# Gated linear attention and a feed-forward layer: keys and queries transposed into scratch tiles in token pairs, growth products over alpha

## The chip, the core and the metric

The kernel runs on one core of a Trainium2 chip. The metric is device time in microseconds (us), the median of several runs. Besides, one execution was taken with the hardware profiler; all views of the profile come from that one execution.

## The reference

Attention comes first, for 4 batches, 8 heads, 768 tokens and a head size of 48, and a feed-forward layer over its 3072 tokens (width 384, hidden width 2048) follows:

```python
for t in range(S):
    state = alpha[:, :, t, :, None] * state + einsum('bhd,bhe->bhde', k[:, :, t], v[:, :, t])
    y[:, :, t] = einsum('bhd,bhde->bhe', q[:, :, t], state)
x = y.transpose(0, 2, 1, 3).reshape(B * S, H * D)
h = x @ w_in
g = h * clip(h + 3.0, 0.0, 6.0) / 6.0
out = g @ w_out
```

The inputs arrive as float64, handed over as their bits, and the chip turns the weights into fp32. alpha lies between 0.8 and 1. All products are fp32.

## The kernel before

**Chunks.** Attention is worked in 24 chunks of 128 tokens, six to a batch. Inside a chunk the recurrence becomes products: keys are multiplied by decay products R (of all alphas from a token to the chunk's end), queries by growth products P. R comes from a scan over alpha backwards (`decay`, L309), followed by a small reciprocal of its first column into a tile `ini` (L313). P comes from a forward scan over alpha that starts from `ini` (`growth`, L320). Both scans run on VectorE. Heads are held in four pairs; alpha, `ini` and P lie as four runs of W = 129 floats, the first of each run being a zero in alpha (the start of the run, which the scan resets at), and `ini` holding a value there and zeros elsewhere.

**Getting the tokens into the free dimension.** alpha, k and q must have tokens along the free dimension. The first six chunks are turned by TensorE (L282). From chunk 6 on (`FIRST`), loads put each of them into a "quad" tile in an order of tokens by which VectorE's transposes of 32 x 32 blocks do the turning (`by_blocks`, L286): four blocks v of a quad are written interleaved, token u of block v to place 4u + v, so that each write goes 16 bytes beyond the last. Then `scaled` (L332) multiplies k by R and q by P, in place, in the tiles `Ks` and `Qs`, of which there are two each, taken in turns by chunk. Keys are needed by token too: `turn_k` (L391) transposes the scaled keys in blocks back into the quad tile, and SyncE's queue writes that to DRAM (`write_k`, L396) and reads it back in another order (`read_k`, L404).

**The rest of a chunk.** Scores are TensorE products of scaled keys and queries (L346), masked by VectorE (L356); ScalarE copies the queries beside them (`place_q`, L366; it does nothing for the first half of a batch's first chunk). GpSimd (POOL) decays the state (L409) by R's first column, ScalarE places it beside the values (L419), TensorE makes the update (L430), VectorE the next state (L438, L440), TensorE the outputs (L456), and ScalarE copies them (L465) to be the feed-forward layer's input.

**Feed-forward.** Two chunks are a group, of which there are twelve. The first groups use plain products (L479, L490, L517), the gate by ScalarE (L495) and VectorE (L499). From the third group on they use products in fewer multiplications: sums of blocks by VectorE (L540, L542, L544, L650, L667), TensorE products (L603 and L706), and ScalarE copies of what is kept (L609).

**Weights.** In the first 80 us or so, the weights are converted: among the steps, ScalarE (L186), VectorE (`high_bits`, L203 to L210, whose last operation reads and writes the odd words of pairs of 32-bit words), and an add on POOL (`add_low`, L217). Loads of the first two quads of each kind are preceded by small memsets on POOL (L257).

**Order.** All the work is issued in one order, written out by hand as a list of words, each a step with its arguments. Each engine runs its instructions in that order, and waits where its data or its tile isn't ready. Words that matter here: `r.j` decay, `p.j` growth, `tk.j` and `tq.j` the transposes of keys and queries, `k.j` and `q.j` the multiplies, `kt.j`, `kw.j` and `kr.j` the way of the keys through DRAM, `st.j` the decayed state on POOL, `sm.j` next state, `sv.j` placing it, `qa.j` placing queries, `la`, `lk`, `lq` loads of alpha, k and q, `d3.i` and `d4.i` the weights' high bits and POOL add, `fr` and `fg` gate steps on ScalarE and VectorE, `xc.g`, `o.g`, `s.g`, `M.g`, `P.g` sums and products of a feed-forward group. `b` is the plain second product, `ca.j` the transpose of alpha, `n.g` a kept copy. A chunk's `tk`, `k`, `kt`, `tq` and `q` stand among the feed-forward words of earlier groups.

Of the kernel before, what the change touches and what calls it, by code (L numbers as in the profile page):

```python
# [8 lines left out]
FP = mybir.dt.float32  # L9
# [8 lines left out]
def kernel(  # L18
# [86 lines left out]
    aX, ini = [], []  # L105
    for r in range(2):
        t = consts.tile([C, NP * W + 1], FP, tag=f"ax{r}")
        nc.vector.memset(t, 0.0)
        aX.append(t)
        t = consts.tile([C, NP * W], FP, tag=f"ini{r}")  # L110
        nc.vector.memset(t, 0.0)
        ini.append(t)
# [114 lines left out]
    Ps = consts.tile([C, NP * W], FP, tag="P", name="P")  # L227
# [46 lines left out]
    def transposed(name, j, i=None):  # L274
        if j >= FIRST:
            t = (K_t if name == "k" else Q_t)[j] = (Ks if name == "k" else Qs)[j % 2]
            by_blocks(t, name, j)
            return
        t = bank("t" + name, j, i)
        src = ring[name, j % NR]  # L280
        for p in range(NP):
            nc.tensor.transpose(  # L282
                t[:, p], src[:, 2 * p : 2 * p + 2].rearrange("s h d -> s (h d)"), ident)

    def by_blocks(to, name, j):
        nc.vector.transpose(out=to.rearrange("r p (u v) -> r p v u", v=V),  # L286
                            in_=quads[name, j % NQ][:, :, :, 0:BLK])
# [16 lines left out]
    def decay(j):  # L304

        n = NP * W
        ax, ic = aX[j % 2], ini[j % 2]
# [5 lines left out]
        nc.vector.reciprocal(out=ic.rearrange("r (p w) -> r p w", w=W)[:, :, 0:1],  # L313
                             in_=R_t[j][:, :, 0:1])

    def growth(j):

        n = NP * W
        P_t[j] = Ps
        nc.vector.tensor_tensor_scan(  # L320
            out=P_t[j], data0=aX[j % 2][:, 0:n], data1=ini[j % 2], initial=0.0,
            op0=ALU.mult, op1=ALU.add)

    def scaled(name, j):

        if j < FIRST:
            src = ps_t.pop(("t" + name, j))
            t = (Ks if name == "k" else Qs)[j % 2]
        else:
            src = t = (K_t if name == "k" else Q_t)[j]  # L330
        by = R_t[j][:, :, 1:W] if name == "k" else without_first(P_t.pop(j))
        nc.vector.tensor_tensor(out=t, in0=src, in1=by, op=ALU.mult)  # L332
        (K_t if name == "k" else Q_t)[j] = t
# [423 lines left out]
    with tc.manual_schedule():  # L757
# [16 lines left out]
               f.1.7.0 r.6 f.1.3.3 d4.8 d2.4 w.10 tk.5.3 d4.9 w.11 dx.4 fr.1.7.1 sm.4.0 d3.4 w.12  # L774
               d2.10 qa.4.0 fg.1.7 fr.1.3.1 m.4 lq.5 d1.10 f.1.6.0 d3.10 d1.12 d4.4 fr.1.0.0 f.1.2.1
               p.5 fg.1.3 d2.12 k.5 fg.1.0 d3.12 d4.10 fr.1.6.1 sm.4.1 tq.5.1 sv.4.1 lk.6 w.13
# [37 lines left out]
               kw.11 M.4.11 G.3.2.1 h.4.0 tq.11 e.4.1.1 la.13 sm.10.1 tk.12 qa.12.0 sv.10.1 M.4.18.0  # L814
               P.3.4 n.4.18.12 q.11 kr.11 sv.12.0 M.4.19 G.3.1.3 o.4.6.0 n.4.11.8 M.4.12 o.4.5.0
               st.11 k.12 qa.10.1 u.11.0 lq.12 h.4.1 qa.11.1 sv.11.0 sm.11.0 tq.12 sc.11.1.2 sv.11.1
               la.14 n.4.12.14 kt.12 P.3.6 M.4.6.2 qa.11.0 o.4.3.0 G.3.3.2 M.4.13 m.11 n.4.13.14
               ca.13 kw.12 ya.11.1 yb.11 cy.11 ya.10.2 o.4.2.0 qa.18.0 o.4.2.1 e.4.2.1 o.4.3.1 yb.10
               M.4.15.1 p.12 cy.10 M.4.16 q.12 xc.5.1 M.4.14 e.4.3.0 xc.5.0 xc.5.3 o.4.4.0 lk.13
               O.3.3 xc.5.4 h.4.3 xc.5.5 kr.12 O.3.1 P.4.0.2 M.5.0.0 o.4.6.1 xc.5.6 e.4.4.0 xc.5.7  # L820
               xc.5.2 M.4.17 h.4.4 lv.13.2 h.4.2 e.4.5.0 n.5.0.14 o.4.7.0 e.4.6.1 u.12.3.0 sc.12.3.0
# [27 lines left out]
               O.5.3 M.7.2 sc.16.3.2 u.16.3.0 qa.16.1 r.17 k.17 r.18 n.7.2.11 G.6.0.0 M.7.3 kt.17  # L849
               h.6.5 M.7.4 n.7.4.15 s.6.1.9 O.4.1 P.6.3.0 tk.18 qa.16.0 s.6.2.12 xc.7.10 M.7.5 K.6.2  # L850
               kw.17 s.6.4 o.7.0.0 k.18 sm.16.0 la.19 s.6.3.8 n.7.5.9 M.7.9 e.7.0.0 kr.17 tq.17
               P.6.2 M.7.18.2 o.7.1.0 sv.16.1 p.17 s.6.5 lk.19 kt.18 O.5.1 M.7.10 sm.16.1 q.17 P.6.5
# [4 lines left out]
               n.7.13.8 o.7.2.0 M.7.16 cy.17 G.6.1.2 cy.16 xc.8.1 M.7.14 q.18 xc.8.3 lq.19 xc.8.4  # L857
               xc.8.10 o.7.6.1 o.7.2.1 e.7.6.1 xc.8.5 e.7.2.0 P.6.6 xc.8.6 G.6.3.1 o.7.4.0 xc.8.0
               xc.8.7 h.7.6 O.5.2 xc.8.8 M.8.0.3 M.7.17 M.8.7.1 O.6.1 o.7.7.1 h.7.2 sm.18.0 n.8.0.11
               n.8.7.8 M.8.1 e.7.3.1 n.8.1.12 r.19 e.7.7.0 xc.8.9 sm.18.1 P.7.0.0 k.19 la.20 K.7.0.2  # L860
               st.19 lk.20 M.8.8 la.21 tq.19 h.7.7 M.8.2 h.7.3 n.8.2.9 e.7.4.1 h.7.4 kt.19 lv.19.0
               sv.19.0 P.7.1 s.7.0.14 M.8.3 M.8.4 G.7.0.2 s.7.1.10 P.7.3.2 xc.8.2 s.7.2.13 kw.19
               n.8.4.15 o.8.0.0 M.8.9 s.7.3.14 kr.19 lk.21 p.19 ca.20 P.7.2 la.22 o.8.1.0 q.19
               e.8.0.1 M.8.10 O.6.3 sc.18.1.3 sc.19.2.0 u.19.1.3 s.7.5 qa.18.1 s.7.4 K.7.2 K.7.1
               tk.20 e.8.1.0 n.8.10.10 h.8.0 M.8.5 lq.20 sv.18.1 lq.21 M.8.11 n.8.11.14 P.7.5
               qa.19.1 M.8.12 h.8.1 sm.19.0 ca.21 n.8.12.9 m.18 n.8.5.13 P.7.4 r.20 qa.19.0 tq.20
               m.19 lv.20.1 M.8.6.3 sv.19.1 M.8.13 G.7.2.1 M.8.18.2 ya.18.2 n.8.13.15 k.20 o.8.3.0
               tk.21 sm.19.1 n.8.18.9 G.7.1.3 ya.19.1 yb.18 yb.19 O.7.2 o.8.3.1 kt.20 o.8.2.0 cy.19
               cy.18 M.8.14 e.8.3.1 o.8.2.1 xc.9.1 O.7.0 h.8.3 P.7.6 xc.9.3 xc.9.4 G.7.3.2 o.8.6.0
               xc.9.0 xc.9.5 M.8.15.3 e.8.2.1 la.23 xc.9.6 o.8.6.1 xc.9.10 st.20 e.8.6.0 o.8.7.0  # L870
               xc.9.7 M.8.16 kw.20 xc.9.8 M.9.0.0 h.8.6 P.8.0.1 kr.20 o.8.4.0 xc.9.9 n.9.0.15 p.20
               O.7.3 M.8.19 e.8.4.0 q.20 h.8.2 lk.22 M.9.1 h.8.4 o.8.5.0 M.8.17 qa.20.0 u.20.1.2
               n.9.1.9 e.8.5.0 o.8.7.1 e.8.7.1 h.8.5 sc.20.1.0 r.21 M.9.7.2 K.8.0.3 sm.20.0 M.9.2
               P.8.1 h.8.7 n.9.7.13 n.9.2.8 sm.20.1 s.8.0.10 G.8.0.1 sv.20.0 M.9.3 p.21 s.8.1.12
               M.9.8 sv.20.1 s.8.2.11 M.9.4 m.20 tk.22 n.9.4.14 k.21 P.8.3.3 o.9.0.0 kt.21 qa.20.1
               xc.9.2 e.9.0.0 s.8.4 M.9.5 st.21 h.9.0 M.9.9 s.8.3.14 o.9.1.0 K.8.2 tq.21 P.8.2 ca.22
               kw.21 lq.22 s.8.5 lv.21.0 kr.21 q.21 n.9.5.12 r.22 K.8.1 M.9.18.0 M.9.10 qa.21.0
               P.8.5 e.9.1.1 n.9.18.14 lv.23.2 sv.21.0 p.22 G.8.2.2 tq.22 ca.23 O.6.0 k.22 kt.22
               n.9.10.10 r.23 qa.21.1 P.8.4 M.9.11 u.21.3.2 sc.21.1.0 n.9.11.11 M.9.15.3 sm.21.0
               M.9.12 G.8.1.0 lk.23 ya.20.3 yb.20 m.21 sm.21.1 sv.21.1 h.9.1 tk.23 n.9.12.8 o.9.6.0  # L880
               cy.20 ya.21.1 yb.21 M.9.19 o.9.5.0 kw.22 M.9.16 M.9.13 o.9.3.0 M.9.6.0 O.8.0 o.9.4.0
               cy.21 n.9.13.8 xc.10.1 e.9.4.1 M.9.17 xc.10.3 o.9.7.0 q.22 lv.22.1 o.9.3.1 qa.22.1
               M.9.14 P.8.6 qa.22.0 st.22 kr.22 xc.10.0 u.22.1.2 O.8.1 o.9.2.0 xc.10.4 G.8.3.1
               o.9.2.1 e.9.3.0 xc.10.5 o.9.7.1 h.9.3 o.9.6.1 e.9.2.0 xc.10.10 h.9.4 M.10.0.0 O.8.2
               n.10.0.8 xc.10.6 P.9.0.1 M.10.1 e.9.7.1 K.9.0.3 xc.10.8 h.9.2 k.23 xc.10.7 e.9.6.0
               h.9.6 e.9.5.0 s.9.0.13 P.9.1 n.10.1.9 kt.23 h.9.5 h.9.7 sm.22.0 O.8.3 M.10.7.2 lq.23
               G.9.0.0 s.9.1.12 sv.22.0 M.10.2 P.9.3.3 s.9.4 s.9.2.10 n.10.2.14 xc.10.2 M.10.3 kw.23
               tq.23 sv.22.1 s.9.3.13 s.9.5 O.7.1 M.10.4 kr.23 p.23 n.10.7.11 M.10.8 P.9.2 n.10.4.15
               q.23 K.9.1 sm.22.1 o.10.0.0 K.9.2 M.10.9 u.23.3 sc.23.1.0 o.10.1.0 qa.23.0 sc.22.3.2
               m.22 M.10.10 P.9.4 st.23 sm.23.0 n.10.10.12 M.10.11 n.10.11.10 e.10.1.0 e.10.0.1  # L890
               M.10.5 h.10.0 P.9.5 qa.23.1 n.10.5.15 G.9.1.1 M.10.12 P.9.6 n.10.12.13 o.10.3.0
               M.10.13 xc.10.9 sv.23.1 G.9.3.2 G.9.2.3 m.23 M.10.15.0 M.10.6.1 n.10.13.13 M.10.18.3
               h.10.1 M.10.16 o.10.2.0 O.9.3 n.10.18.13 o.10.7.0 o.10.2.1 o.10.3.1 sv.23.0 ya.22.3
               yb.22 ya.23.2 yb.23 cy.22 cy.23 e.10.3.1 o.10.6.0 o.10.4.0 O.9.1 xc.11.1 M.10.14
               M.10.19 o.10.6.1 e.10.2.0 o.10.5.0 h.10.2 xc.11.3 M.10.17 e.10.5.0 xc.11.4 O.9.2
# [45 lines left out]
```

## Time and profile before

| | before |
|---|---|
| Median of 3 runs | 533.77 us (533.75 to 533.82) |
| Profiled execution, own time | 533.63 us |
| Its span | 531.82 us |
| TensorE matmul busy | 524.3 us (99%) |
| TensorE weight load busy | 494.0 us (93%) |
| VectorE busy | 475.6 us (89%) |
| ScalarE busy | 261.4 us (49%) |
| GpSimd (POOL) busy | 50.3 us (9%) |
| Granted TensorE clock | 1.00 throughout |

The span is from the first to the last instruction; 1.81 us of the execution's own time lie outside it. In the profile PE is TensorE's matmul, PEld its weight load, DVE VectorE, ACT ScalarE, POOL GpSimd and SP SyncE, whose queue issues the transfers; L12 is line 12 of the kernel. A group gives line, engine, operation, output and input tiles by name, shapes and count, then busy time and the mean of one in ns, then the idle time before and what ended it. A line of the timeline gives start, duration, engine, line, operation and, in brackets, the idle time before it with what ended that. Tiles are called by the names in the program: `q<-qq` is a transpose from a quad of queries, `kq<-k` the one of `turn_k`, `k<-k,R` a multiply, `t_ps` and `m_ps` are PSUM.

### The profile page before, as it was taken

The numbers are of one execution on the slowest core, as the hardware profiler recorded it, in microseconds if no ns is written. First come the engines' busy times: TensorE is split into PE (matmuls) and PEld (weight loads), VectorE is DVE, ScalarE is ACT, GpSimd is POOL, SyncE is SP. The second block draws the span as 40 slices with busy tenths as digits, with TensorE's granted clock in tenths as the row PEclk, the third lists the DMA queues.
The fourth block names the chain that finished last, engine by engine and source line by source line (L and its number), as shares of the span: only waits on it lengthen the run. The fifth ranks groups of instructions, "written<-read, shape, count | busy, mean of one in ns | idle before, by whom it ended". The sixth has DMA issues, their size and how long they took to land.

```text
span 531.8 us, 15076 instructions
## 1 busy us (share of the span) xinstructions
PE 524.3 (99%) x6290; PEld 494.0 (93%) x6290; DVE 475.6 (89%) x839; ACT 261.4 (49%) x513; POOL 50.3 (9%) x71
## 2 busy tenths in 40 slices
PE   8999999999999999999999999999999999999997
PEld 5798886789999999999999999999999999999997
DVE  7999999999999999999999999998999999486471
ACT  4888875212664453542673554544454454443330
POOL 5333353100000100000000000000000000000000
PEclk9999999999999999999999999999999999999999
DMA  9999867005363253453463553443531532010000
GB/s 177 246 241 251 247 153 177 2 2 133 74 150 84 64 118 77 115 123 89 95 156 85 120 136 91 96 107 69 145 78 20 129 98 48 1 33 7 9 17 30
DMA packets 124100, 54.40 MB, mean 102 GB/s; under 512 B 83328, under 2 KB 116864, under 8 KB 124032
## 3 DMA queue, kind: packets, MB, share of 16 engines
q1 hardware_dynamic: 124032, 53.44, 42.2%
q8 instruction: 49, 0.80, 0.7%
q14 instruction: 19, 0.16, 0.1%
HBM read 44.50 MB, written 8.91 MB: 100 GB/s over the span
## 4 chain that ended last, share of the span: by engine, by line
PE 85%; DVE 7%; ACT 4%; DMA 1%; issue 1%; SPq 1%; POOL 0%; DVEq 0%; ACTq 0%
PE m_ps L706 36%; PE m_ps L603 31%; PE m_ps L479 4%; PE m_ps L517 4%; PE t_ps L456 4%; PE t_ps L346 2%; PE t_ps L430 2%; DMA rings<-in_q_dram 1%; DVE A L356 1%; ACT A L366 1%; DVE g_sb L540 1%; ACT r L495 1%; ACT raw L186 1%; DVE g_sb L499 1%; SPq L251 1%
## 5 line engine op out<-in xcount | busy, mean ns | idle before, releaser
L706 PE MATMUL m_ps<-w,g_sb 128*128 128x192 f32 x704 | 121.7, 326 | 0.0
L609 ACT COPY g_sb<-m_ps 128x512 f32<-128x512 f32 x110 | 63.5, 584 | 104.2 <-PE m_ps L603 86.4
L706 PEld LDWEIGHTS m_ps<-w,g_sb 128*128 128x128 f32 x704 | 113.7, 190 | 0.6 <-DVE g_sb L667 0.3
L706 PE MATMUL m_ps<-rings,g_sb 128*128 128x192 f32 x528 | 91.7, 327 | 0.2 <-DVE g_sb L650 0.2
L706 PEld LDWEIGHTS m_ps<-rings,g_sb 128*128 128x128 f32 x528 | 85.3, 190 | 0.6 <-DVE g_sb L650 0.5
L603 PE MATMUL m_ps<-xc,w 128*128 128x128 f32 x640 | 83.5, 277 | 0.0
L603 PEld LDWEIGHTS m_ps<-xc,w 128*128 128x128 f32 x640 | 77.9, 192 | 1.1
L495 ACT ACTIVATE r<-g_sb,half 128x512 f32<-128x512 f32 x80 | 57.0, 722 | 29.8 <-DVE g_sb L499 11.9
L499 DVE SCALAR_TENSOR_TENSOR g_sb<-r,g_sb 128x512 f32<-128x512 f32 x80 | 53.5, 682 | 8.7 <-ACT r L495 8.4
L603 PE MATMUL m_ps<-xT,raw 128*128 128x128 f32 x400 | 52.8, 277 | 0.0
L603 PEld LDWEIGHTS m_ps<-xT,raw 128*128 128x128 f32 x400 | 48.8, 192 | 0.5 <-ACT g_sb L609 0.2
L409 POOL TENSOR_TENSOR st<-sm,R 128x192 f32<-128x192 f32 x20 | 12.6, 630 | 358.2 <-DVE sm L440 300.5
L650 DVE TENSOR_TENSOR g_sb<-g_sb 128x512 f32<-128x512 f32 (+1 forms) x55 | 42.1, 792 | 3.7 <-PE m_ps L706 3.5
L603 PE MATMUL m_ps<-xT,w 128*128 128x128 f32 x320 | 42.0, 277 | 0.0
L603 PEld LDWEIGHTS m_ps<-xT,w 128*128 128x128 f32 x320 | 39.0, 192 | 0.4
L366 ACT COPY A<-q 48x256 f32<-48x256 f32 x88 | 35.4, 403 | 7.3 <-DVE q L332 6.1
L356 DVE TENSOR_TENSOR A<-t_ps,mask 64x256 f32<-64x256 f32 x96 | 36.2, 416 | 1.2 <-PE t_ps L346 0.8
L479 PE MATMUL m_ps<-xT,w 128*128 128x256 f32 x144 | 33.3, 384 | 0.5 <-POOL w L217 0.3
L603 PE MATMUL m_ps<-xc,raw 128*128 128x128 f32 x240 | 32.1, 277 | 0.1
L479 PEld LDWEIGHTS m_ps<-xT,w 128*128 128x128 f32 x144 | 26.5, 190 | 5.3 <-POOL w L217 0.9
L540 DVE TENSOR_TENSOR g_sb<-g_sb 128x512 f32<-128x512 f32 x40 | 27.2, 682 | 4.6 <-ACT g_sb L609 4.6
L309 DVE TENSOR_TENSOR_SCAN R<-t,ones 128x516 f32<-128x516 f32 x24 | 29.6, 1233 | 1.6 <-ACT t L300 1.6
(105 smaller groups left out, 726.9 us busy)
## 6 DMA issues: line engine op xcount, KB each, us to landing
raw<-in_moe_w_out_dram SPq DMA_DIRECT2D x8, 768.0 KB, 5.5
raw<-in_moe_w_in_dram SPq DMA_DIRECT2D x6, 768.0 KB, 7.3
v<-in_v_dram SPq DMA_DIRECT2D x48, 96.0 KB, 3.1
out_dram<-oh SPq DMA_DIRECT2D x44, 96.0 KB, 1.8
far<-kq SPq DMA_DIRECT2D x64, 64.0 KB, 2.2
kb<-far SPq DMA_DIRECT2D x64, 64.0 KB, 2.0
aq<-in_alpha_dram SPq DMA_DIRECT2D x36, 96.0 KB, 2.5
kq<-in_k_dram SPq DMA_DIRECT2D x36, 96.0 KB, 2.5
```

Source lines behind the costliest of these rows:

```text
L309: nc.vector.tensor_tensor_scan(out=reverse(R, n - 1, n), data0=reverse(ax, n, n), data1=reverse(ones, n, n), initial=0.0, op0=ALU.mult, op ...
L356: nc.vector.tensor_tensor(out=to[:, a], in0=sc[a][half], in1=mask[half, half].unsqueeze(1).to_broadcast([HB, NP, HB]), op=ALU.mult)
L366: nc.scalar.copy(out=to[:, a], in_=Q_t[j][64 * a : 64 * a + D, :, half])
L456: nc.tensor.matmul(y_of(j, (i + 1) // 2, p)[:, HB * b : HB * b + HB], vb[:, p, e : e + 32], A_t[j][:, b, 2 * p + a], start=(b == 0 and i = ...
L479: nc.tensor.matmul(h[:, f], w1[:, kk, o : o + C], xT_t[g][:, kk], start=(kk == 0), stop=(kk == KT - 1))
L495: nc.scalar.activation(out=to, in_=h, func=AF.Relu, bias=half, scale=1.0 / 6.0)
L499: nc.vector.scalar_tensor_tensor(out=to, in0=r, scalar=1.0, in1=h, op0=ALU.min, op1=ALU.mult)
L540: eng.tensor_tensor(out=out, in0=in0, in1=in1, op=ALU.add if s1 > 0 else ALU.subtract)
L603: nc.tensor.matmul(acc[g][i][:, f * C : (f + 1) * C], spots[w][:, f * C : (f + 1) * C], x_of(g, x), start=(first and f == 0), stop=last, s ...
L609: nc.scalar.copy(out=slots[z], in_=acc[g][i])
L650: nc.vector.tensor_tensor(out=out, in0=in0, in1=in1, op=ALU.subtract)
L706: nc.tensor.matmul(to[g], a, rhs[:, f], start=(first and f == 0), stop=(last and f == HF - 1), skip_group_check=True)
```

## The change

1. `tk.j` and `tq.j` of chunks 6 on no longer write `Ks` and `Qs` but scratch tiles (`turns`), one for keys and one for queries. In scratch the tokens lie in two halves, w = 0 and 1, which are 1 KB apart; each half holds pairs (4u + 2w, 4u + 2w + 1), so that a transpose writes every second float, 8 bytes beyond the last.
2. The multiplies of these chunks read scratch in pairs (two floats, then two from the other half), the growth or decay products and the output `Ks` or `Qs` contiguously in the same order.
3. The growth scan of chunks 6 on writes over its input alpha; chunks before that write the queries' scratch tile, and the tile P of its own is gone. Since the scan overwrites the four zeros that start the runs of alpha, a memset of 4 columns on POOL follows each such scan (18 of them) and sets them to zero again.
4. There is one `ini` tile in place of two, and one memset less at the start. So growth j must be issued before decay j + 1, and multiply k.j before tk.(j + 1).
5. The list of words is the same up to the places of some: r.6 moves behind p.5; r.18 and k.18 move behind p.17, ahead of s.6.5; tk.22 moves behind k.21; qa.12.0 and qa.18.0, which do nothing, move too. TensorE's and ScalarE's own orders stay as they were.

```diff
-    aX, ini = [], []
+    aX = []
     for r in range(2):
         t = consts.tile([C, NP * W + 1], FP, tag=f"ax{r}")
         nc.vector.memset(t, 0.0)
         aX.append(t)
-        t = consts.tile([C, NP * W], FP, tag=f"ini{r}")
-        nc.vector.memset(t, 0.0)
-        ini.append(t)
+    ini = consts.tile([C, NP * W], FP, tag="ini")
+    nc.vector.memset(ini, 0.0)
...
-    Ps = consts.tile([C, NP * W], FP, tag="P", name="P")
+    places = {name: consts.tile([C, NP * W], FP, tag=f"{name}t", name=f"{name}t")
+              for name in "kq"}
+    turns = {name: t[:, 0 : NP * C].rearrange("r (w p n) -> r w p n", w=2, p=NP)
+             for name, t in places.items()}
...
     def transposed(name, j, i=None):
         if j >= FIRST:
-            t = (K_t if name == "k" else Q_t)[j] = (Ks if name == "k" else Qs)[j % 2]
-            by_blocks(t, name, j)
+            nc.vector.transpose(
+                out=turns[name].rearrange("r w p (u b) -> r p w b u", b=V // 2),
+                in_=quads[name, j % NQ].rearrange("r p (w b) d -> r p w b d", w=2)[..., 0:BLK])
             return
...
     def growth(j):
-        P_t[j] = Ps
-        nc.vector.tensor_tensor_scan(
-            out=P_t[j], data0=aX[j % 2][:, 0:n], data1=ini[j % 2], initial=0.0,
-            op0=ALU.mult, op1=ALU.add)
+        P_t[j] = places["q"] if j < FIRST else aX[j % 2]
+        to = P_t[j][:, 0:n]
+        nc.vector.tensor_tensor_scan(out=to, data0=aX[j % 2][:, 0:n], data1=ini, initial=0.0,
+                                     op0=ALU.mult, op1=ALU.add)
+        if j >= FIRST:
+            nc.gpsimd.memset(to.rearrange("r (p w) -> r p w", w=W)[:, :, 0:1], 0.0)
...
     def scaled(name, j):
+        t = (K_t if name == "k" else Q_t)[j] = (Ks if name == "k" else Qs)[j % 2]
+        by = R_t[j][:, :, 1:W] if name == "k" else without_first(P_t.pop(j))
         if j < FIRST:
-            src = ps_t.pop(("t" + name, j))
-            t = (Ks if name == "k" else Qs)[j % 2]
-        else:
-            src = t = (K_t if name == "k" else Q_t)[j]
-        by = R_t[j][:, :, 1:W] if name == "k" else without_first(P_t.pop(j))
-        nc.vector.tensor_tensor(out=t, in0=src, in1=by, op=ALU.mult)
-        (K_t if name == "k" else Q_t)[j] = t
+            nc.vector.tensor_tensor(out=t, in0=ps_t.pop(("t" + name, j)), in1=by, op=ALU.mult)
+            return
+        pairs = lambda x: x.rearrange("r p (u w b) -> r p u w b", w=2, b=V // 2)
+        nc.vector.tensor_tensor(
+            out=pairs(t), in0=turns[name].rearrange("r w p (u b) -> r p u w b", b=V // 2),
+            in1=pairs(by), op=ALU.mult)
...
-               f.1.7.0 r.6 f.1.3.3 d4.8 ...
...
-               p.5 fg.1.3 d2.12 k.5 fg.1.0 d3.12 d4.10 ...
+               ... p.5
+               r.6 fg.1.3 d2.12 k.5 fg.1.0 d3.12 d4.10 ...
...
-               ... qa.16.1 r.17 k.17 r.18 n.7.2.11 ...
-               ... s.6.4 o.7.0.0 k.18 sm.16.0 ...
-               ... o.7.1.0 sv.16.1 p.17 s.6.5 lk.19 kt.18 ...
+               ... qa.16.1 r.17 k.17 n.7.2.11 ...
+               ... s.6.4 o.7.0.0 sm.16.0 ...
+               ... o.7.1.0 sv.16.1 p.17 r.18 k.18 s.6.5 lk.19 kt.18 ...
...
-               p.21 s.8.1.12 ... m.20 tk.22 n.9.4.14 k.21 P.8.3.3 ...
+               p.21 s.8.1.12 ... m.20 n.9.4.14 k.21 tk.22 P.8.3.3 ...
```

## The prediction

> **What bounds it now.** The first part of the page and its chain of waits (columns: busy us, share of the span, instructions):
>
> ```profile
> PE 524.3 (99%) x6290; PEld 494.0 (93%) x6290; DVE 475.6 (89%) x839; ACT 261.4 (49%) x513; POOL 50.3 (9%) x71
> PE 85%; DVE 7%; ACT 4%; DMA 1%; issue 1%; SPq 1%; POOL 0%; DVEq 0%; ACTq 0%
> ```
>
> TensorE sets the end. The change takes nothing from it and leaves its order alone, so it can only alter TensorE's waits. The busy time of the stretch in which nearly all the edited instructions run (us; PE, PEld, DVE, ACT and POOL busy; granted clock, DMA share, GB/s), and TensorE's longest waits from 76 us on (total, times, longest):
>
> ```profile
> 140.00:452.00 312.00, 311.65 (x3999) 305.52 (x3988) 301.03 (x543) 152.96 (x322) 9.80 (x16) 1.00 0.43 100
> PEld m_ps L706 <- DVE g_sb L650: 0.5, 1, 0.5
> PEld m_ps L603 <- DVE xc L542: 0.4, 1, 0.4
> PEld m_ps L706 <- DVE g_sb L667: 0.3, 1, 0.3
> ```
>
> Of 312 us PE works 311.65 and VectorE 301.03: VectorE is nearly as full, yet TensorE hardly ever waits for it. Next, the groups by shape: what the change makes cheaper (first, second), the multiplies behind them (third, fourth), and two rows by which I price it (busy us, mean ns, idle before).
>
> ```profile
> L286 DVE STREAM_TRANSPOSE q<-qq 128x512 f32<-128x512 f32 x18 | 20.1, 1118 | 0.1
> L286 DVE STREAM_TRANSPOSE k<-kq 128x512 f32<-128x512 f32 x18 | 20.1, 1116 | 0.5 <-PE t_ps L346 0.4
> L332 DVE TENSOR_TENSOR k<-k,R 128x512 f32<-128x512 f32 x18 | 12.3, 685 | 0.1
> L332 DVE TENSOR_TENSOR q<-q,P 128x512 f32<-128x512 f32 x18 | 12.2, 681 | 0.2
> L391 DVE STREAM_TRANSPOSE kq<-k 128x512 f32<-128x512 f32 x16 | 11.2, 698 | 0.1
> L210 DVE SCALAR_TENSOR_TENSOR raw<-raw,w 128x768 uint32<-128x768 uint32 x11 | 10.6, 960 | 0.4
> ```
>
> **1. Cheaper transposes: 15.1 us of VectorE.** A quad's transpose writes every fourth float (16 bytes apart): 1118 ns. L391, the same operation writing contiguous rows, takes 698, so the 16-byte step costs 0.42. The new writes go to every second float. L210 reads and writes every second word, and its 960 ns for 768 elements is the contiguous rate (681 for 512: 1.33 ns an element against 1.25). So 0.70 each, 36 x 0.42 = 15.1 us less.
>
> **2. Multiplies that read pairs.** No row reads two floats and then jumps 1 KB. Nearest is again L210's half-dense access at full rate: 0.68, no change. The upper bound is the 16-byte step's price, +0.42 each, which would eat the whole saving; a gain is excluded, the contiguous multiply being as fast as any row. [...]
>
> **3. Term C, what TensorE can get of the 15 us.** Only its waits, start to start over the normal step (0.163 at L706, 0.112 at L603): 0.24 at 151.17 (on DVE L542), 0.26 at 152.57 (landing of a kb read, whose queue waits for the transpose of turn_k at L391), 0.19 at 155.66 (ScalarE's L609 behind DVE), 0.14 at 241.82, 0.34 at 411.44, 0.11 at 424.67, 0.08 at 429.5: 1.36. The first two lie behind one cheaper q transpose, 0.42 at most together; that makes 1.28, and I take C = -1.2. The vanished ring wait (0.40 ahead of tk.19, in L286's second row) and one memset less at the start (489 ns, VectorE idle there) fall in idle time: zero. tk.22 behind k.21: zero.
>
> **4. Term A, r.6 behind p.5.** With one `ini`, decay 6 must follow growth 5, so the hand-written order puts it there. VectorE and POOL before:
>
> ```profile
> 62.38 1.21 DVE L309 TENSOR_TENSOR_SCAN R<-t,ones 128x516 f32<-128x516 f32 x1
> 65.28 0.67 DVE L499 SCALAR_TENSOR_TENSOR g_sb<-r,m_ps 128x512 f32<-128x512 f32 x1
> 69.49 1.23 DVE L320 TENSOR_TENSOR_SCAN P<-t 128x516 f32<-128x516 f32 x1
> 69.71 2.27 POOL L217 TENSOR_TENSOR w<-raw 128x768 int32<-128x768 int32 x1 [2.36 <-ACT r L495]
> 71.96 0.68 DVE L499 SCALAR_TENSOR_TENSOR g_sb<-r,m_ps 128x512 f32<-128x512 f32 x1
> 72.78 5.69 PE L479 MATMUL m_ps<-xT,w 128*128 128x256 f32 x24 [0.18 <-DVE g_sb L499]
> ```
>
> Scan and reciprocal hold 63.71 - 62.38 = 1.33. Taken out, what follows moves up only 0.58, because the gate at 65.28 needs ScalarE's r, which ends at 64.68. p.5 then starts at 68.91, r.6 at 70.17 (+1.26), the next gate at 71.50 (+1.33) instead of 70.75. So fg.1.3, k.5 and fg.1.0 end 0.75 later, and the last is what PE waits for at 72.78: no cover, +0.75. What r.6 itself serves comes later and has cover.
>
> POOL comes on top. A scan and POOL's add hold one another:
>
> ```profile
> 49.63 1.47 POOL L217 TENSOR_TENSOR w<-raw 128x768 int32<-128x768 int32 x1 [3.25 <-DMA aq<-in_alpha_dram]
> 49.91 2.28 DVE L320 TENSOR_TENSOR_SCAN P<-t 128x516 f32<-128x516 f32 x1
> 246.09 1.59 DVE L650 TENSOR_TENSOR g_sb<-g_sb 128x512 f32<-128x512 f32 x2
> 246.33 0.80 POOL L409 TENSOR_TENSOR st<-sm,R 128x192 f32<-128x192 f32 x1 [29.22 <-DVE sm L440]
> ```
>
> The scan at 49.91 began during a POOL add that ended at 51.10, and ended 1.09 after it, as if it had started then: 2.28 in place of 1.2. At 246.33 the waiting POOL instruction got in between two operations of VectorE, and the pair took 1.59, against 1.24 for the same pair at 331.06 (below). In the changed order d4.10 starts 0.13 after L210, at 69.13, waits through p.5 (68.91 to 70.14), and runs 1.26 beyond the scan's end, to 71.40 (as 71.98 - 70.72 before). r.6 is also a scan with two SBUF inputs and comes just there: it ends 1.09 after 71.40, at 72.49 instead of 71.39. Before, the gate stood there, which reads PSUM. +1.10; A = 0.75 + 1.10 = +1.85. [...]
>
> **5. Term B, r.18 and k.18 behind p.17.** They leave 1.95 us ahead of o.7.1.0 (329.31), which gains only 0.16: it waits for the L603 group that ends at 329.08. p.17 is then at 329.77, r.18 with reciprocal (1.13 behind, 1.35 long) and k.18 (0.60) follow, and s.6.5 (the two L650) starts at 332.85, not 331.06.
>
> ```profile
> 331.06 1.24 DVE L650 TENSOR_TENSOR g_sb<-g_sb 128x512 f32<-128x512 f32 x2
> 333.19 2.58 PEld L706 LDWEIGHTS m_ps<-w,g_sb 128*128 128x128 f32 x16
> ```
>
> The first half ends at 333.51; +0.11 to a load (72.64 to 72.75) is 333.62 against 333.19: B = +0.43. kt.18, sm.16.1, q.17 and SP's kw.18 and kr.18 behind them come up to 1.8 later; that has cover, as tq.18 and tk.19 save 0.84 and the ring wait 0.40.
>
> **6. Term D, the POOL memset between p and q.** The trace has no such wait; its parts are there: VectorE to POOL 0.17 (sm to L409), a POOL memset 0.10 to 0.15, POOL to VectorE 0.03: 0.35, less the present gap of 0.03. In 13 of 18 chunks 1.1 us or more lie between p and q; in five (10, 12, 15, 20, 23) q follows at once: 5 x 0.3 = 1.5 us of VectorE, hidden by the 0.84 that each chunk saves; if that cover is gone, 1.5. On POOL's own queue a decayed state waits behind a memset in chunks 9, 14, 15 and 16 (slack least at 16, 1.1 us), and d4.11 comes about 1 later (slack 4, at PE 84.67). DMAs wait for none of them. Zero.
>
> **Sum.** A 1.85 + B 0.43 - C 1.2 + D 0 = +1.08. The profiled execution took 533.63 (span 531.82 and 1.81 outside), 0.14 under the median: 534.7 by its own time, 534.9 by the median. Less than 0.2% (1.07 us) can't be told from no change; the bounds are 532.70 and 534.84.
>
> **Rivals.**
> - *POOL's add does not hold r.6* (it may be let in earlier, or finish ahead). A is 0.75: 533.8. For it: at 69.71 the overlap with p.5 delayed POOL only. Chance 0.15, no change.
> - *The moves cost TensorE nothing* and C is paid out: 533.77 - 1.2 = 532.6, the other side. Its place is PE 72.78, and it decides if VectorE's order ahead of fg.1.0 closes up by 0.75 more than the 0.58 I found. Against it: VectorE is dense from 65.3 to 72.6. Chance 0.10. Full pay of 15 us is excluded, as PE has no such waits.
> - *Paired reads pay +0.42 each.* VectorE gains nothing, C goes, and D's 1.5 is partly open: 533.77 + 2.28 + 0 to 1 = 536.0 to 537. As a whole, VectorE becomes the bound only when a multiply costs some 0.72 more: idle 11.0 of the stretch, plus 32 x 0.42 = 13.4 saved, less D's 1.5, over 32. Chance 0.15.
> - *It doesn't do what it says*: the transposes stay at 1.12 because the price lies in gathering the input, strided in the quad as before. Against: L391's input is strided too. Also C lost, D open: 536 to 537.5. Chance 0.07.
> - My forecast holds the rest, 0.53, own range 534.3 to 535.4; it lies on the bound, 0.33 slower and 0.20 within.
>
> **How the numbers follow.** Slower 0.33 + 0.15 + 0.07 = 0.55; same 0.20 + 0.15 = 0.35; faster 0.10. The range 533.5 to 536.5 takes in the second case and most of the paired-read one, and leaves out the faster case and the far ends.
>
> **What would show it.** In the profile after: k and q transposes near 0.70, multiplies near 0.68 (1.1 would be the fourth case); VectorE's busy time down by about 14 (15.1 and the memset's 0.5, less 1.1 while r.6 is held); a decay scan near 70.2 lasting over 2 us beside L217; PE's wait ahead of the 72.78 group up by 1.85 (by 0.75 if POOL lets it pass); a new wait of about 0.4 for L650 near 335; the waits at 152 and 411 gone. I am wrong if that group starts no later, or if TensorE starts waiting for q products.

## The result, and the profile after

The changed kernel took 535.69 us (median of 6 runs, 535.06 to 536.53) against 533.75 (6 runs, 533.05 to 533.82): a ratio of 1.0039, interval 1.0026 to 1.0052. Timed again beside some of the experiments below it took 534.62 (8 runs, 533.81 to 536.38) against 533.39 (25 runs, 532.63 to 534.54): 1.0026, 1.0014 to 1.0039. It is slower, by 1.2 to 1.9 us. Its single times lie wider apart than those of the kernel before; why, is part of the answer.

The page of the changed kernel, and below it its stretch from 140 to 452 us (PE, PEld, DVE, ACT, POOL busy; clock, DMA share, GB/s):

```profile
PE 525.5 (98%) x6290; PEld 496.2 (93%) x6290; DVE 465.4 (87%) x838; ACT 261.8 (49%) x513; POOL 50.5 (9%) x89
```

```profile
140.00:452.00 312.00, 311.88 (x4070) 305.95 (x4069) 293.25 (x547) 154.86 (x325) 10.76 (x31) 1.00 0.43 101
```

VectorE lost 10.2 us of work over the whole span; TensorE, which sets the end, was busy only 0.2 us more of the 312 in this stretch. The groups by shape (busy us, mean ns, idle before):

```profile
L337 DVE TENSOR_TENSOR q<-qt,t 128x512 f32<-128x512 f32 x18 | 12.7, 707 | 1.1 <-POOL t L327 1.1
L278 DVE STREAM_TRANSPOSE qt<-qq 128x512 f32<-128x512 f32 x18 | 12.7, 704 | 0.1
L278 DVE STREAM_TRANSPOSE kt<-kq 128x512 f32<-128x512 f32 x18 | 12.6, 701 | 0.1
L337 DVE TENSOR_TENSOR k<-kt,R 128x512 f32<-128x512 f32 x18 | 12.3, 684 | 0.1
```

The transposes do what the change says (1118 to 704 ns), and reading pairs costs the multiplies nothing that counts (681 and 685 before). The one new wait in these rows is the memset's: 1.1 us in all.

The time went elsewhere. The timeline around 70 us (start, duration, engine; idle time before and what ended it in brackets):

```profile
64.12 0.69 DVE L505 SCALAR_TENSOR_TENSOR g_sb<-r,m_ps 128x512 f32<-128x512 f32 x1 [0.67 <-ACT r L501]
68.34 1.23 DVE L324 TENSOR_TENSOR_SCAN qt<-t,ini 128x516 f32<-128x516 f32 x1
68.56 2.27 POOL L216 TENSOR_TENSOR w<-raw 128x768 int32<-128x768 int32 x1 [3.13 <-ACT raw L185]
69.48 2.43 DVE L312 TENSOR_TENSOR_SCAN R<-t,ones 128x516 f32<-128x516 f32 x1
72.16 0.69 DVE L505 SCALAR_TENSOR_TENSOR g_sb<-r,m_ps 128x512 f32<-128x512 f32 x1
73.37 0.68 DVE L505 SCALAR_TENSOR_TENSOR g_sb<-r,m_ps 128x512 f32<-128x512 f32 x1
74.19 7.11 PE L485 MATMUL m_ps<-xT,w 128*128 128x256 f32 x24 [2.19 <-DVE g_sb L505]
```

Scan 6, now behind growth scan 5, took 2.43 and ended 1.08 after POOL's add; the gates behind it came late, and TensorE waited 2.19 us where it had waited 0.18. And then a second loss: the same 24 products took 7.11 where they had taken 5.69. Three stretches of 3.4 us show why (columns as above):

```profile
71.40:74.80 3.40, 1.21 (x8) 0.95 (x7) 3.30 (x7) 1.82 (x4) 0.00 (x0) 1.00 0.79 280
74.80:78.20 3.40, 3.40 (x10) 2.69 (x9) 3.37 (x6) 2.56 (x4) 1.47 (x1) 0.51 0.82 120
78.20:81.60 3.40, 3.40 (x18) 2.88 (x17) 3.33 (x6) 1.38 (x3) 0.42 (x4) 0.99 0.72 258
```

After a stretch in which TensorE was busy for 1.21 of 3.4 us, the granted clock stood at a half for the next one (0.51), though TensorE was then fully busy, and returned to full. Product to product the step went from 0.216 to 0.427 and back.

Near 335 the moved r.18 and k.18 show as forecast, smaller:

```profile
332.93 1.21 DVE L312 TENSOR_TENSOR_SCAN R<-t,ones 128x516 f32<-128x516 f32 x1
334.85 1.29 DVE L656 TENSOR_TENSOR g_sb<-g_sb 128x512 f32<-128x512 f32 x2
335.59 2.57 PEld L712 LDWEIGHTS m_ps<-w,g_sb 128*128 128x128 f32 x16 [0.24 <-DVE g_sb L656]
```

TensorE runs the same products in the same order in all these kernels, so one can ask by how much each is later. The table gives that, in us against the kernel before, counted from the product that stands at 68.55 there. At that product the executions of the table stand between 0.83 us earlier and 0.05 us later than the kernel before, whether r.6 was moved or not; the difference is there by 60 us, ahead of all moved words, and is left out in this way. The columns are one profiled execution each of the changed kernel and of kernels of the next section.

| at (before) | changed | r.6 early | all moves undone | r.6 behind k.5 | only r.6 moved | only r.18, k.18 moved |
|---|---|---|---|---|---|---|
| 72.78, start of the group | 2.00 | -0.15 | 0.00 | 0.78 | 2.00 | -0.01 |
| 78.31, its last product | 3.42 | -0.15 | 0.00 | 0.77 | 3.42 | -0.01 |
| 157.96 | 2.91 | -0.66 | -0.31 | 0.26 | 3.41 | -0.03 |
| 245.02 | 2.70 | -0.88 | -0.51 | 0.03 | 3.40 | -0.03 |
| 331.96 | 2.67 | -0.91 | -0.55 | 0.15 | 3.37 | 1.00 |
| 336.08 | 2.98 | -0.59 | -0.54 | 0.47 | 3.37 | 1.31 |
| 424.48 | 2.71 | -0.86 | -0.82 | 0.20 | 3.35 | 1.81 |
| last product | 2.54 | -0.93 | -1.00 | 0.03 | 3.30 | 1.83 |

### The profile page after: what moved, and what is told of

Read it like the earlier page. It is cut to its first block, busy times and chain, and to the rows that moved or that the text cites. A ratio compares the mean times of both kernels' runs of the same rounds, so it can differ in the third digit from the quotient of the medians.

```text
span 533.8 us, 15098 instructions
## 1 busy us (share of the span) xinstructions
PE 525.5 (98%) x6290; PEld 496.2 (93%) x6290; DVE 465.4 (87%) x838; ACT 261.8 (49%) x513; POOL 50.5 (9%) x89
## 4 chain that ended last, share of the span: by engine, by line
PE 88%; DVE 6%; ACT 3%; issue 1%; DMA 0%; POOL 0%; SPq 0%; DVEq 0%; ACTq 0%; POOLq 0%
PE m_ps L712 37%; PE m_ps L609 32%; PE m_ps L523 4%; PE m_ps L485 4%; PE t_ps L462 4%; PE t_ps L352 2%; PE m_ps L540 2%; PE t_ps L436 2%; DVE A L362 1%; PE t_ps L285 1%; DVE R L312 1%; ACT r L501 1%; ACT A L372 1%; DVE g_sb L505 1%; ACT w L195 1%
## 5 line engine op out<-in xcount | busy, mean ns | idle before, releaser
L609 PEld LDWEIGHTS m_ps<-xT,w 128*128 128x128 f32 x320 | 39.0, 192 | 0.4
L485 PE MATMUL m_ps<-xT,w 128*128 128x256 f32 x144 | 34.7, 397 | 2.6 <-DVE g_sb L505 2.2
L485 PEld LDWEIGHTS m_ps<-xT,w 128*128 128x128 f32 x144 | 27.8, 198 | 7.5 <-issue 2.4
L312 DVE TENSOR_TENSOR_SCAN R<-t,ones 128x516 f32<-128x516 f32 x24 | 30.8, 1284 | 2.7 <-ACT t L303 2.7
L609 PEld LDWEIGHTS m_ps<-xc,raw 128*128 128x128 f32 x240 | 29.8, 192 | 0.2
```

The source lines that it names most:

```text
L312: nc.vector.tensor_tensor_scan(out=reverse(R, n - 1, n), data0=reverse(ax, n, n), data1=reverse(ones, n, n), initial=0.0, op0=ALU.mult, op ...
L485: nc.tensor.matmul(h[:, f], w1[:, kk, o : o + C], xT_t[g][:, kk], start=(kk == 0), stop=(kk == KT - 1))
L609: nc.tensor.matmul(acc[g][i][:, f * C : (f + 1) * C], spots[w][:, f * C : (f + 1) * C], x_of(g, x), start=(first and f == 0), stop=last, s ...
```

## The experiments

**Theory:** r.6's new place makes TensorE wait, POOL's add accounts for over half of that, and the wait takes down the clock. **Rivals:** the clock falls for another reason; or the cost is in the new operations, the scratch tiles, pair reads and memset waits.

**r.6 early again.** The scan goes back to its old place; only its reciprocal, which writes the single `ini`, stays behind p.5 (a new word `ri`).

```diff
-        nc.vector.reciprocal(out=ini...[:, :, 0:1], in_=R_t[j][:, :, 0:1])
+        if j not in (6,):
+            start_growth(j)        # the reciprocal; also the step of the word ri
...
-  f.1.7.0 f.1.3.3 ... p.5 r.6 fg.1.3
+  f.1.7.0 r.6 f.1.3.3 ... p.5 ri.6 fg.1.3
```

> Changed kernel, but decay scan 6 stands early again (behind f.1.7.0); only its reciprocal, which writes the single ini tile, stays behind p.5. Theory (the moved scan makes TensorE wait 2.19 us ahead of the L485 group at 74.2, and that wait brings the granted clock down to a half, 1.42 us more): the wait falls to about 0.2 to 0.3, the clock stays 1.00, and the time falls by some 2.8 to 532.8 to 533.0. Rival 1 (the clock falls for another reason than the wait): only the wait's 1.4 comes back, 534.2, clock still 0.997. Rival 2 (the cost is in the new operations: memset waits, pair reads): 535.2 or more.

Measured: 532.56 (11 runs) against 533.24 (30 runs), 0.9985, 0.9976 to 0.9994; 0.7 below the kernel before. The group's wait is gone, and the clock was 0.999 or 1.00 in all eleven. The time lies 0.2 under the range that I had expected. The theory holds; both rivals needed 534 or more.

**All moves undone.** The same, and r.18 and k.18 at their old places, with reciprocal 18 behind p.17. ("All" means these three: tk.22 stays behind k.21, as the one scratch tile demands, and so do qa.12.0 and qa.18.0, which do nothing, at their new places.)

```diff
-  r.17 k.17 n.7.2.11 ... o.7.0.0 sm.16.0 ... p.17 r.18 k.18 s.6.5
+  r.17 k.17 r.18 n.7.2.11 ... o.7.0.0 k.18 sm.16.0 ... p.17 ri.18 s.6.5
```

> Changed kernel with r.6, r.18 and k.18 all at their old places, their reciprocals 6 and 18 behind p.5 and p.17. Theory: as the run with r.6 alone, and 0.2 to 0.3 better, since s.6.5 stands 1.8 earlier again: 532.5 to 532.8, that is 1.0 to 1.2 under the kernel before, which is what the cheaper transposes are worth to TensorE (term C). Rival (memset waits and pair reads cost TensorE what the transposes save): 533.5 to 534.

Measured: 532.27 (11 runs) against 533.24, 0.9980, 0.9971 to 0.9989, so 1.0 below the kernel before. It beats both kernels: the cheaper transposes are a gain, of the size of term C, and the moved words turn it into a loss. That scratch tiles and memset waits eat it is ruled out. Against r.6 alone it is 0.3 better, as in the table from 332 to 336 (0.31), though the two times by themselves overlap. The ends of the two columns lie only 0.07 apart: up to 158 both kernels have the same order and yet stand 0.35 apart, so a single profile can be off by that much.

**The wait filled.** Products of the identity, five times 128 columns, stand on TensorE between tq.5.1 and f.1.4.2.

```diff
-  sm.4.1 tq.5.1 sv.4.1
+  sm.4.1 tq.5.1 zi.2.5 sv.4.1      # 5 x 128 columns into a free bank
```

> Changed kernel with five 128-column products of the identity put on TensorE between tq.5.1 and f.1.4.2 (about 2.1 us), into a PSUM bank that nothing uses there. The wait for fg.1.0 stays as long; only TensorE is busy in it. Theory (the idle 2.2 us lower the clock): clock 1.00, the L485 group takes 5.6 instead of 7.1, and the time is 1.2 to 1.5 below the changed kernel, 534.2. Rival (the clock is lowered by something else, such as the load of transfers at 74 to 76): the group still takes about 7, time 535.5 to 535.8.

Measured: 534.55 (8 runs) against 533.24, 1.0025, 1.0014 to 1.0035. All eight had a clock of 1.00. The profile of the filled kernel:

```profile
70.38 2.43 DVE L312 TENSOR_TENSOR_SCAN R<-t,ones 128x516 f32<-128x516 f32 x1
72.73 1.25 PE L744 MATMUL t_ps<-ident 128*128 128x512 f32 x4
75.09 5.69 PE L485 MATMUL m_ps<-xT,w 128*128 128x256 f32 x24 [1.11 <-DVE g_sb L505]
```

Scan 6 is held as before and the group starts as late behind the products ahead of it (72.30 to 75.09 here, 71.41 to 74.19 there). But with the filler TensorE idles for 1.11 instead of 2.19, the clock stays up, and the group takes 5.69 again. So the idle time lowers the clock, not the load of transfers, which is about the same (a DMA share of 0.80 and then 0.86 in two stretches of 3.4 us from 72.30, against 0.79 and 0.82 above). At the group's last product this kernel is 2.00 later than the kernel before, where the changed kernel is 3.42 later: the difference of 1.42 is the clock's. The filler took 1.25 and not the 2.1 that I had expected. The median is 1.3 above the kernel before, about what the changed kernel shows in executions without the drop (0.9 in the second set, below); that 1.4 is saved can't be read from medians, because the changed kernel loses it only in some of its executions.

**r.6 behind k.5.**

```diff
-  p.5 r.6 fg.1.3 d2.12 k.5 fg.1.0
+  p.5 fg.1.3 d2.12 k.5 r.6 fg.1.0
```

> Changed kernel with r.6 three words later, behind fg.1.3 and k.5 and still ahead of fg.1.0. VectorE has the same work ahead of fg.1.0, but r.6 no longer stands where POOL's L216 add runs. Theory (POOL's add holds the scan for 1.1 to 1.2): r.6 takes 1.25 instead of 2.43, TensorE's wait falls from 2.19 to about 1.0, and if a wait of 1.0 leaves the clock alone the time is 533.1, if it lowers it 534.5. Rival (r.6 is long for another reason, such as its reversed read of alpha just written): it stays about 2.4 and the time 535.5.

Measured: 533.34 (11 runs) against 533.24, 1.0004, 0.9996 to 1.0013; with the clock up, 533.1 was expected.

```profile
68.32 2.27 POOL L216 TENSOR_TENSOR w<-raw 128x768 int32<-128x768 int32 x1 [3.12 <-ACT raw L185]
69.36 0.69 DVE L505 SCALAR_TENSOR_TENSOR g_sb<-r,m_ps 128x512 f32<-128x512 f32 x1
70.57 1.22 DVE L312 TENSOR_TENSOR_SCAN R<-t,ones 128x516 f32<-128x516 f32 x1
72.73 5.68 PE L485 MATMUL m_ps<-xT,w 128*128 128x256 f32 x24 [0.96 <-DVE g_sb L505]
```

POOL's add ends at 70.59, the scan now starts there and takes 1.22; the gate that stood under the add reads PSUM and took 0.69. TensorE waits 0.96, and the group starts 0.78 later than before: close to the part of term A (0.75) that is order, without the hold. The clock stays up, and the rival (a scan that is long by itself) is out.

**The moves alone, on the kernel before.** One word, then two, and nothing else of the change.

```diff
-  f.1.7.0 r.6 f.1.3.3 ... p.5 fg.1.3
+  f.1.7.0 f.1.3.3 ... p.5 r.6 fg.1.3
```

> Kernel before with one word moved, r.6 behind p.5, nothing else of the change (two ini tiles, old transposes, no memsets). Theory: scan 6 takes 2.4 beside POOL's L217, TensorE's wait ahead of the L479 group grows from 0.18 to about 2.0 to 2.2, the clock falls to a half for some 3.4 us, and the time is 2.5 to 3.2 above the kernel before. Rival (the cost comes with scratch tiles, pair reads or memsets): within 0.3 of the kernel before.

Measured: 535.80 (6 runs) against 533.39, 1.0048, 1.0032 to 1.0064: 2.4 above, just under the expected 2.5 to 3.2, with the lower clock in three of the six. Scan, group and wait are those of the changed kernel to within a hundredth:

```profile
69.41 2.43 DVE L309 TENSOR_TENSOR_SCAN R<-t,ones 128x516 f32<-128x516 f32 x1
74.12 7.11 PE L479 MATMUL m_ps<-xT,w 128*128 128x256 f32 x24 [2.18 <-DVE g_sb L499]
```

So one moved word by itself makes a loss larger than the change's, as nothing is given back later (last row of the table, 3.30 against 2.54).

```diff
-  k.17 r.18 ... o.7.0.0 k.18 ... p.17 s.6.5
+  k.17 ... o.7.0.0 ... p.17 r.18 k.18 s.6.5
```

> Kernel before with r.18 and k.18 moved behind p.17, nothing else. Theory: s.6.5 starts some 1.7 later, TensorE waits 0.2 to 0.4 for it at L706 near 333, and the time is 0.3 to 0.4 above the kernel before; with the old, longer transposes behind it nothing is given back. Rival (there is cover): no wait there, time unchanged.

Measured: 534.48 (11 runs) against 533.39, 1.0015, 1.0007 to 1.0024: 0.8 above by the ratio, 1.1 by the medians, more than expected. The wait for s.6.5 is there (0.24, and 0.31 in the table at 336). Some 0.5 more follows by 424, where the changed kernel loses nothing, and 0.4 of it is one wait, on a copy of ScalarE behind VectorE's gate:

```profile
341.00 0.67 DVE L499 SCALAR_TENSOR_TENSOR g_sb<-r,g_sb 128x512 f32<-128x512 f32 x1
341.77 0.59 ACT L609 COPY g_sb<-m_ps 128x512 f32<-128x512 f32 x1 [3.24 <-DVE g_sb L499]
342.41 0.97 PEld L603 LDWEIGHTS m_ps<-xc,w 128*128 128x128 f32 x8 [0.32 <-ACT g_sb L609]
```

Between s.6.5 and this gate stand two of the old transposes, 1.10 each, where the changed kernel has 0.71 and 0.70 and TensorE no wait. Another 1.0 of this profile lies ahead of the moved words:

```profile
275.05 0.16 PEld L430 LDWEIGHTS t_ps<-v,kb 64*48 64x48 f32 x2 [0.34 <-DMA kb<-far]
275.86 0.26 PEld L430 LDWEIGHTS t_ps<-v,kb 64*48 64x48 f32 x13 [0.65 <-DMA kb<-far]
```

A read of keys from DRAM landed late. No word moved ahead of this place, so it is chance: in the second profile of the changed kernel the same place is 0.4 late, with the wait filled 0.2, with r.6 behind k.5 0.1, elsewhere nothing. The profiled execution is also the slowest of the eleven (535.50). How much of the measured 0.8 to 1.1 is such chance stays open.

**The changed kernel again**, beside these three:

> The changed kernel unaltered, timed beside the other runs of this set. Theory (a wait of about 2.2 us ahead of the L485 group that lowers the clock in most executions, by a window whose place differs from run to run): 1.7 to 2.2 above the kernel before, single times spread by more than 1 us, and a mean clock of 0.996 to 0.998 in most of them. Rival (a lasting cost in the new operations): the same mean, but no such spread of the clock.

Measured: the 534.62 told at the start, 1.2 above the kernel before and so less than the expected 1.7 to 2.2; the spread is there. Two of eight executions had a mean clock of 0.997 over the span (536.38 and 535.48), the others 1.00 (533.81 to 535.42, median 534.25). In the first set it was five of six (0.996 or 0.997), with r.6 alone moved three of six: 10 of 20 together, while all 19 executions with r.6 behind k.5 or the wait filled (0.96 and 1.11 us idle) had 0.999 or 1.00. So the wait of 2.19 brings the drop about every second time, not mostly, as I had expected.

**Memset behind q**, on top of all moves undone.

```diff
-        if j >= FIRST:                       # in growth
-            nc.gpsimd.memset(to...[:, :, 0:1], 0.0)
+        if name == "q":                      # in scaled, behind the multiply
+            nc.gpsimd.memset(aX[j % 2]...[:, :, 0:1], 0.0)
```

> As the run with all moves undone, and POOL's memset of the four columns is issued behind the multiply of q and not ahead of it, so that q waits for nothing on POOL (the memset then has until the next transpose of alpha into that tile, two chunks on). Theory (the five memset waits, 1.1 us in all on VectorE, are hidden behind the cheaper transposes): VectorE's idle time for L327 is gone and the time the same as with the moves undone within 0.2, 1.0 below the kernel before. Rival (they cost TensorE): 0.5 or more below that run.

Measured: 532.65 (11 runs) against 533.39, 0.9987, 0.9973 to 1.0000. With the moves undone, VectorE's list of waits has the first of these lines, and with the memset behind q none for that multiply, which then takes 681 ns:

```profile
DVE q L341 <- POOL t L331: 1.1, 5, 0.3
```

```profile
L339 DVE TENSOR_TENSOR q<-qt,t 128x512 f32<-128x512 f32 x18 | 12.3, 681 | 0.2
```

The waits are gone and the time is not better: 0.7 below the kernel before, where 1.0 was expected, and the intervals of the two overlap. No cost of these waits to TensorE shows. (One execution of these eleven, 535.73, had a clock of 0.997, though its order has no long wait that would explain it; it was not the profiled one, and its cause is open.)

## Why the prediction was right, and what it lacked

The sign came out as forecast and by the steps given. In the profiled execution the sum by table is 2.54, of which 1.42 is the clock; the rest is 1.12 where the prediction's sum was 1.08. So close a sum is partly luck: A was 0.15 too small and B 0.12 too large. In the second profile of the changed kernel the last product is 3.00 later, 0.37 of it the late read of keys at 275.

- **Term A (1.85) measured 2.00.** Parts: the gate at 65.28 moved up 0.57 against TensorE's own products (0.58 forecast) and stopped at ScalarE's r, as said (0.67 idle, `ACT r`); scan 6 ended 1.08 after POOL's add (1.09 forecast); 0.78 remains without the hold. The missing 0.15 is in the small steps between scan, reciprocal and gate. The rows with r.6 at its two places (2.43 beside the add, 1.22 behind it) show that the scan waited for the add's end, and that, held, it then needed only 1.08.
- **The step that was missing is the clock.** The prediction let a longer wait cost its own length. It cost 1.42 more in the profiled executions in which the clock fell. With five drops in six the first set lies at 535.69, above the forecast's own range of 534.3 to 535.4; with two in eight the second lies inside, at 534.62. That the range of 533.5 to 536.5 held the 535.69 is luck: it was made that wide for rivals that did not come true, not for the clock.
- **Term B (0.43) measured 0.31**, and the cover for what comes later held in the changed kernel; with the old transposes some 0.5 more was lost, 0.4 of it not at the key transfers that the prediction named but at a copy of ScalarE behind VectorE's gate (342.41 above).
- **Term C (1.2) measured 1.19** in the changed kernel (0.51 by 158, 0.21 by 245, 0.03 by 332, 0.27 from 336 to 424, 0.17 by the end), and 1.00 with the moves undone. The change's real worth is that, as only these few waits of TensorE were there to be had.
- **Term D (1.5, hidden) measured 1.1**, in five places, hidden.
- **The 15.1 us of VectorE were mis-sized**, without effect on the sum. In the timeline durations overlap with the next instruction's start, those of the old transposes more: from start to start a transpose went from 0.96 to 0.63, which is 36 x 0.33 = 11.9, and VectorE's busy time fell by 10.2 where 14 was forecast.
- **Pair reads** cost nothing (684 and 707, and 681 with the memset behind q); the rival that priced them at 0.42 is out, and so is the one in which the transposes stay slow.

## What to carry to other kernels

Where the bounding engine hardly waits, a change that cheapens another engine is worth only the bounding engine's few waits (here 1.19 us, of the 10.2 taken off VectorE), and an order that has to give way for it can cost more (here 2.00 and 0.31 of waiting, and 1.42 of clock). When an order must change because two steps now share a tile, move only the instruction that touches the tile: here the 0.1 us reciprocal instead of the 1.2 us scan, which turned 1.2 to 1.9 us of loss into 1.0 of gain. Price a new wait of TensorE not by its length alone, but also by the slower clock that may follow (here 1.42 us behind a wait of 2.19, in half of the executions).

## What the runs showed of the hardware

An idle time of 2.2 us on TensorE was followed by half the granted clock, for 3.41 us in the profile of the changed kernel (74.85 to 78.26), and the span's mean clock shows such a drop in 10 of 20 executions; 0.96 and 1.11 us brought none in 19. Three of the ten were profiled, and in each the wait was 2.18 or 2.19 and the group behind it took 7.11. In the changed kernel the whole wait lay in the 3.41 us just ahead of the drop, and TensorE had been busy for only 1.22 us of them (71.44 to 74.85). With only r.6 moved it was busy for 1.22 of 3.40 (71.30 to 74.70, mean clock 0.94), and the next 3.40 had a mean clock of 0.55. In the traces of the changed kernel and of the kernel before, the records of the granted clock begin 6.58 and 4.43 us into the span. A last one behind the span's end left out, they are 68.27, 3.41 and 457.39 us long in the one and 529.07 in the other, which is 20, 1, 134 and 155 times 3.413.

Counted on in such steps, the least busy stretches with no drop behind them had 2.07 us of work (528.82 to 532.24 in the changed kernel) and 2.28 (526.67 to 530.08 in the kernel before); in the filled one, a stretch of 3.40 with 2.29 of work (72.30 to 75.70) had a clock of 1.00, and so had the next two. So, as an estimate from these numbers, the limit lies somewhere between 1.22 and 2.07 of 3.41 us; no run places it closer. That the other ten executions escaped because two such steps shared the wait would fit, but is not shown: none of them was profiled.
